# Nystrom attention and gated MLP on one core: identity products placed in other PSUM tiles, and four weight tiles of the second pair decoded elsewhere in ScalarE's order

## The chip, the cores and the metric

One core of a Trainium2 chip runs the whole program. The metric is the device time of one execution in microseconds; lower is better. The kernel before takes 792.78 us, the median of three runs (792.62 to 793.05).

## What is computed

Eight batches of eight heads, 576 tokens and 64 channels go through Nystrom attention with 32 landmarks, and the result, 4608 rows of 512, through a gated MLP of width 1536:

```python
q_lm, k_lm = means of q and k over 18 neighbouring tokens
A, Bm, C = softmax(q k_lm'), softmax(q_lm k_lm'), softmax(q_lm k')
Z = Bm' / (norm1(Bm) * norminf(Bm) + 1e-6)
for _ in range(6):
    Z = 2 * Z - Z @ Bm @ Z
x = A @ Z @ C @ v
xn = x / sqrt(mean(x * x) + 1e-6) * rms_g
out = (silu(xn @ w_gate) * (xn @ w_val)) @ w_out
```

## The kernel before

The program works batch by batch. For a batch the attention front makes the scores of the landmarks (`sC`, `sA`), exponentials (`E`, `tA`), the six Newton steps (`pn`, `PV`) and a small matrix `W`. The row norm needs the squares of `x` (`pO` on TensorE, `sq` on ScalarE), their sums (`pss`), which VectorE transposes (`sqT`), and a second small product (`pms`), from which a chain of VectorE operations (`ms`, `r`) makes the factor of each row. The scaled `AT` is split into a high and a low part, `an`.

The MLP does not multiply `x` by the gate and value weights directly. For each pair of 128-wide slices it first mixes the weights with the attention's matrix `WT` (`pM`, in `mix_weights`, L298), splits that into `Mhi` and `Mlo`, and then takes `an` times these: twelve products for each of four blocks of a pair, six into a gate bank `psg` and six into a value bank `psv`. ScalarE takes the SiLU of the gate bank (`s`, L533), VectorE multiplies by the value bank (L534). Three pairs make a half of the MLP, after which `outs` (L542) multiplies by `w_out` (`pso`).

Weights arrive as raw bytes and are decoded on the chip. `Weights.begin` (L177) puts two ScalarE operations on a tile (L195 and L197) and returns a function that puts the closing VectorE operation (L205). Four tiles make a pair of gate and value weights; the tiles of the first pair are `wgv0`, of the second `wgv1`, of the third `wgv2`. `opening` (L818) lays out batch 0 by hand: what is wrapped in `own` or `pin` keeps the order in which it is written, and the closing functions wait in the list `ends` until they are popped. `steady` (L966) then feeds the work of batch 1 into the first MLP chunk (`mlp`, L495), at block counts that `until` names, beside a stream of further weight tiles (`early.stream`). The order of instructions that nothing pins is set by the scheduler.

Products of the identity with itself have no use in the result; they keep TensorE at work. They go into free columns of a PSUM tile:

```python
        def idle(out, n):
            for _ in range(n):
                mm(out, ident, ident, start=True, stop=True)
```

There are three of them behind the sums of squares in `second` (L1154), in the last columns of the bank of `pss`, and six behind the mixing of the second pair in `mlp` (L512), in the last columns of the value bank `psv` of the block before.

Of the kernel before, what the change touches and what calls it, by code (L numbers as in the profile page):

```python
# [20 lines left out]
P = 128  # L21
# [39 lines left out]
def nystrom_moe_kernel(  # L61
# [53 lines left out]
    def mm(*args, **kw):  # L115
        tc.keep_in_program_order(nc.tensor.matmul(*args, **kw))  # L116
# [165 lines left out]
    def mixed_banks(wts, b, pair, banks=None):  # L282
        wgv = wts.get("gv", pair)
        pool, tag = banks or (pg, "pg")
        ps = [pool.tile([P, 4 * P], F32, name="pM", tag=tag) for g in range(G)]
        for h in range(4):
            for g in range(G):
                n = pos(g, h)
                mm(
                    ps[g][rows(n), :],  # L290
                    WT[half(h), b, 2 * g + h // 2, rows(n % 2)],
                    wgv[half(h), 2 * g + h // 2, :],
                    start=True,
                    stop=True,
                )
        return ps

    def mix_weights(wts, b, pair, late=False, own=free, banks=None):  # L298

        ps = mixed_banks(wts, b, pair, banks)  # L300
# [94 lines left out]
    hs, ends = [], []  # L395
# [99 lines left out]
    def mlp(wts, b, f0, an, store, part, following, after=2 * NF1):  # L495
# [4 lines left out]
        for n, pair in enumerate(pairs):  # L500
# [5 lines left out]
            for i in range(2):  # L506
                s = mp.tile([P, S], F32, name="s", tag="s", bufs=2)
                for e in range(2):
                    if very and i and e and n + 1 < NPAIR:
                        mix_weights(wts, b, pairs[n + 1])  # L510
                        if not n:
                            for _ in range(6):  # L512
                                mm(ps[:, 3 * P :], ident, ident, start=True, stop=True)
                        yield 1.1
# [63 lines left out]
    with tc.tile_pool(name="ap", bufs=1, side="right") as ap, tc.tile_pool(  # L578
# [158 lines left out]
        def expose(b, g, own=free):  # L737
            tA = state[b]["tA"][g]
            own(nc.scalar.activation(tA, tA, AF.Exp, scale=SC))
# [23 lines left out]
# [4 lines that stand above are left out]
# [51 lines left out]
        def opening():  # L818
# [53 lines left out]
            ends.append(early.begin(own))  # L872
# [4 lines left out]
            for _ in range(2):  # L877
                ends.pop(0)()
            next(parts)
            next(parts)  # L880
            for _ in range(2):
                ends.pop(0)()
            nxt.exps()
            next(parts)
            nxt.turned(es=(0,))
# [7 lines left out]
            nxt.turned(es=(1,))  # L893
# [72 lines left out]
        def steady(begun):  # L966
# [9 lines left out]
            expose(1, 0, pin)  # L976
            expose(1, 1, pin)
# [5 lines left out]
            yield 1.3, 0.0  # L983
            mix.add(early.stream(WAIT))
# [143 lines left out]
        def second(b, own=free):  # L1128
# [28 lines left out]
            if not b:  # L1157
                idle(room[:, 512 - P :], 3)
# [288 lines left out]
```

## Time and profile before

| | before |
|---|---|
| median of three runs | 792.78 us |
| profiled execution, time | 793.83 us |
| its span | 792.1 us |
| TensorE busy | 769.8 us (97%) |
| VectorE busy | 561.5 us (71%) |
| ScalarE busy | 418.2 us (53%) |
| mean granted TensorE clock | 0.991 |

The span goes from the first to the last instruction; 1.7 us of the profiled time lie around it. TensorE is busy for nearly all of the span, but not evenly: of the 40 slices of some 20 us on the page, the first three show 7, 7 and 6 tenths for it, every later one 9 and the last 8. A granted clock of 1.00 is 2.4 GHz and 0.50 is 1.2 GHz.

### The profile page before, as it was taken

Reading aid. Unit: us, or ns where it says so; the run is one execution under the profiler, and the core shown is the slowest. Engines: PE = TensorE matmul, PEld = TensorE weight load, DVE = VectorE, ACT = ScalarE, POOL = GpSimd, SP = SyncE. Lnnn points to the kernel's source line nnn. Section 1 sums busy time; section 2 is a strip of 40 time slices with the busy share of each in tenths; the row PEclk is TensorE's granted clock in tenths of the full one; section 3 lists DMA queues with packets and bytes.
Section 4 is the critical chain, followed back from the end, with each engine's and each line's share of the span. In section 5 each row is a group of like instructions: output and inputs, shape, how many; then the busy total and the mean of one; then the engine's idle time right before and its main releaser. Section 6 shows DMA issues by size and latency. Waiting matters only on the chain.

```text
span 792.1 us, 17966 instructions
## 1 busy us (share of the span) xinstructions
PE 769.8 (97%) x7042; PEld 619.4 (78%) x7042; DVE 561.5 (71%) x1325; ACT 418.2 (53%) x927; POOL 197.8 (25%) x211
## 2 busy tenths in 40 slices
PE   7769999999999999999999999999999999999998
PEld 5457768778778778678778879797979797979796
DVE  7696687957969758688577574767476757766672
ACT  4678365534545455464475785555355444535460
POOL 4524120110110200200200004353334424433430
PEclk9979999999999999999999999999999999999999
DMA  9966361541652541521556541334332424151412
GB/s 329 361 214 220 109 218 63 181 134 39 194 183 81 186 140 61 185 95 46 173 168 221 152 143 41 132 94 145 94 143 71 158 81 158 55 182 57 171 41 79
DMA packets 55204, 110.83 MB, mean 140 GB/s; under 512 B 5456, under 2 KB 29008, under 8 KB 55120
## 3 DMA queue, kind: packets, MB, share of 16 engines
q1 hardware_dynamic: 55120, 109.69, 41.1%
q8 instruction: 55, 0.90, 0.5%
q14 instruction: 29, 0.24, 0.1%
HBM read 73.69 MB, written 35.98 MB: 138 GB/s over the span
## 4 chain that ended last, share of the span: by engine, by line
PE 88%; ACT 4%; DMA 3%; DVE 3%; issue 1%; SPq 1%; POOL 1%; ACTq 0%; POOLq 0%
PE pso L116 38%; PE p L116 17%; PE psv L116 9%; PE psg L116 9%; PE pM L116 5%; PE pn L116 2%; PE sC L116 2%; PE pO L116 1%; DMA wrawg<-in_moe_w_gate_dram 1%; PE pCV L116 1%; DMA vt<-in_v_dram 1%; PE pss L116 1%; PE pW L116 1%; PE sE L129 1%; SPq L592 0%
## 5 line engine op out<-in xcount | busy, mean ns | idle before, releaser
L116 PE MATMUL pso<-wo,h 128*128 128x512 f32 x648 | 158.5, 396 | 0.0
L116 PEld LDWEIGHTS pso<-wo,h 128*128 128x128 f32 x648 | 118.6, 188 | 31.5 <-ACT E L685 4.2
L116 PE MATMUL pso<-lhio,h 128*128 128x512 f32 x432 | 139.3, 392 | 0.0
L116 PEld LDWEIGHTS pso<-lhio,h 128*128 128x128 f32 x432 | 81.1, 188 | 23.1 <-issue 5.9
L116 PE MATMUL p<-xb,Bwgv 128*128 128x288 f32 x560 | 90.8, 296 | 0.0
L116 PE MATMUL psg<-an,Mhi 128*128 128x288 f32 x384 | 85.8, 306 | 1.6 <-DVE Mlo L306 1.4
L116 PE MATMUL pso<-lloo,h 128*128 128x512 f32 x216 | 84.4, 391 | 0.0
L116 PE MATMUL psv<-an,Mhi 128*128 128x288 f32 x384 | 82.6, 299 | 0.0
L116 PEld LDWEIGHTS p<-xb,Bwgv 128*128 128x128 f32 x560 | 81.3, 188 | 1.1
L436 POOL TENSOR_TENSOR s<-s,vv 128x576 f32<-128x576 f32 x40 | 57.4, 1434 | 98.2 <-DVE vv L478 96.8
L116 PEld LDWEIGHTS psg<-an,Mhi 128*128 128x128 f32 x384 | 62.1, 190 | 12.9 <-DVE WT L1107 5.0
L116 PE MATMUL p<-xb,Bwo 128*128 128x288 f32 x392 | 70.1, 295 | 0.0
L116 PEld LDWEIGHTS psv<-an,Mhi 128*128 128x128 f32 x384 | 62.2, 189 | 1.8
L735 POOL TENSOR_TENSOR tA<-tA,mA 128x576 f32<-128x576 f32 x16 | 18.7, 1187 | 175.9 <-DVE mA L734 175.9
L1309 ACT COPY ob<-pso 128x512 f32<-128x512 f32 x36 | 21.1, 589 | 75.6 <-PE pso L116 50.7
L116 PEld LDWEIGHTS p<-xb,Bwo 128*128 128x128 f32 x392 | 58.9, 188 | 1.2
L533 ACT ACTIVATE s<-psg 128x288 f32<-128x288 f32 x96 | 39.4, 410 | 38.7 <-PE psg L116 38.5
L116 PE MATMUL psv<-an,Mlo 128*128 128x288 f32 x192 | 59.0, 307 | 0.0
L116 PE MATMUL psg<-an,Mlo 128*128 128x288 f32 x192 | 58.4, 304 | 0.0
L1371 DVE TENSOR_TENSOR obl<-obl,pso 128x512 f32<-128x512 f32 x36 | 24.7, 685 | 43.6 <-PE pso L116 42.9
L534 DVE TENSOR_TENSOR s<-s,psv 128x288 f32<-128x288 f32 x96 | 42.3, 446 | 16.7 <-PE psv L116 11.1
L538 ACT CAST h<-s 128x576 fp32r<-128x576 f32 x48 | 32.2, 670 | 27.5 <-DVE s L534 27.5
(206 smaller groups left out, 1488.6 us busy)
## 6 DMA issues: line engine op xcount, KB each, us to landing
xb<-ad SPq DMA_DIRECT2D x16, 1008.0 KB, 5.2
qk<-in_q_dram SPq DMA_DIRECT2D x16, 576.0 KB, 5.1
qk<-in_k_dram SPq DMA_DIRECT2D x16, 576.0 KB, 6.4
pd<-ob SPq DMA_DIRECT2D x36, 256.0 KB, 3.3
ad<-t SPq DMA_DIRECT2D x64, 144.0 KB, 1.8
obl<-pd SPq DMA_DIRECT2D x36, 256.0 KB, 2.7
out_dram<-obl SPq DMA_DIRECT2D x36, 256.0 KB, 2.0
vt<-in_v_dram SPq DMA_DIRECT2D x16, 512.0 KB, 5.6
```

The lines of the kernel that those rows point to most:

```text
L116: tc.keep_in_program_order(nc.tensor.matmul(*args, **kw))
L129: tc.keep_in_program_order(nc.tensor.transpose(*args))
L436: kept(eng.tensor_mul(ss[f][:, e], ss[f][:, e], vv[f][:, e]))
L533: silu["last"] = nc.scalar.activation(s[:, cols], banks[0], AF.Silu).ins
L534: nc.vector.tensor_mul(s[:, cols], s[:, cols], banks[1])
L538: nc.scalar.copy(h[:, 0, TAIL:], s)
L735: own(nc.gpsimd.tensor_sub(tA, tA, mA.unsqueeze(2).broadcast_to([P, NB, M])))
L1309: nc.scalar.copy(ob, ps)
L1371: kept(nc.vector.tensor_add(ob, ob, ps))
```

## The change

Identity products: the three behind the sums of squares go, the six in the value bank go, and eight new ones are put into the second bank of the mixing (`ps[1]`), ahead of the mixing of the second pair. The second pair's mixing is given priority in the scheduler. Of the second pair's four tiles, the first is decoded behind the exponentials of batch 1's first group instead of ahead of `W`, the second and third follow one place later each, and the fourth goes between the two exponentials `tA` of batch 1. Three closing operations of the first pair stand ahead of the two transposes of the sums, one behind them. The two transposes of batch 1's `sA` (`turned`) come together behind the first half's `an`. The stream of further weight tiles starts at block count 37 of the first chunk.

```diff
-    def mixed_banks(wts, b, pair, banks=None):
+    def mixed_banks(wts, b, pair, banks=None, fill=0):
         ps = [pool.tile([P, 4 * P], F32, name="pM", tag=tag) for g in range(G)]
+        for _ in range(fill):
+            mm(ps[1][:, :P], ident, ident, start=True, stop=True)
         for h in range(4):
...
-    def mix_weights(wts, b, pair, late=False, own=free, banks=None):
+    def mix_weights(wts, b, pair, late=False, own=free, banks=None, fill=0):
-        ps = mixed_banks(wts, b, pair, banks)
+        ps = mixed_banks(wts, b, pair, banks, fill)
...
                     if very and i and e and n + 1 < NPAIR:
-                        mix_weights(wts, b, pairs[n + 1])
-                        if not n:
-                            for _ in range(6):
-                                mm(ps[:, 3 * P :], ident, ident, start=True, stop=True)
+                        with nullcontext() if n else tc.high_priority():
+                            mix_weights(wts, b, pairs[n + 1], fill=0 if n else 8)
                         yield 1.1
...
             back(b, 1, own)
-            ends.append(early.begin(own))
             newton_weights(b, own)
             nxt.tops()
             parts = second(b, own)
             next(parts)
-            for _ in range(2):
+            for _ in range(3):
                 ends.pop(0)()
             next(parts)
             next(parts)
-            for _ in range(2):
-                ends.pop(0)()
             nxt.exps()
             next(parts)
-            nxt.turned(es=(0,))
+            ends.pop(0)()
             ends.append(early.begin(own))
             room = next(parts)
             low_parts = mix_weights(early, 0, 0, True, own, (pa, "pa"))
...
             next(parts)
-            nxt.turned(es=(1,))
+            nxt.turned()
             idle(room, 3)
...
             expose(1, 0, pin)
+            begun.insert(-1, early.begin(pin))
             expose(1, 1, pin)
...
             nxt.totals()
             yield 1.3, 0.0
+            yield from until(0, 37)
             mix.add(early.stream(WAIT))
...
-            if not b:
-                idle(room[:, 512 - P :], 3)
             yield 1.1, SQW
```

On ScalarE at the end of the opening, before (`wrawg2` is the first tile of the second pair, `wgv0` the first pair's weights):

```order
L197 ACTIVATE wgv0_462<-wrawg1_169 128x4x128
L195 ACTIVATE wrawv1_171<-wrawv1_171 128x512
L197 ACTIVATE wgv0_462<-wrawv1_171 128x4x128
L195 ACTIVATE wrawg2_176<-wrawg2_176 128x512
L197 ACTIVATE wgv1_584<-wrawg2_176 128x4x128
L1105 COPY W_592<-pW_587 128x128
```

and now:

```order
L197 ACTIVATE wgv0_462<-wrawg1_169 128x4x128
L195 ACTIVATE wrawv1_171<-wrawv1_171 128x512
L197 ACTIVATE wgv0_462<-wrawv1_171 128x4x128
L1104 COPY W_589<-pW_584 128x128
L1140 ACTIVATE sq_609<-pO_597 128x288
```

The tile `wrawg2` no longer stands ahead of the copy `W`, which the products `pO` read.

On VectorE at the sums of squares (`sqT` are the transposed sums, `ms` the start of the row factors, the four `wgv` rows the closing operations of the first pair), before:

```order
L205 SCALAR_TENSOR_TENSOR wgv_462<-wrawg_165,wgv_462 128x4x128
L205 SCALAR_TENSOR_TENSOR wgv_462<-wrawv_167,wgv_462 128x4x128
L1151 STREAM_TRANSPOSE sqT<-pss 128x288
L205 SCALAR_TENSOR_TENSOR wgv_462<-wrawg_169,wgv_462 128x4x128
L205 SCALAR_TENSOR_TENSOR wgv_462<-wrawv_171,wgv_462 128x4x128
L1151 STREAM_TRANSPOSE sqT<-pss 128x288
L717 STREAM_TRANSPOSE tA<-sA 128x288
L1164 TENSOR_SCALAR ms<-pms 128x18
```

and now:

```order
L205 SCALAR_TENSOR_TENSOR wgv_462<-wrawg_165,wgv_462 128x4x128
L205 SCALAR_TENSOR_TENSOR wgv_462<-wrawv_167,wgv_462 128x4x128
L205 SCALAR_TENSOR_TENSOR wgv_462<-wrawg_169,wgv_462 128x4x128
L1150 STREAM_TRANSPOSE sqT<-pss 128x288 x2
L205 SCALAR_TENSOR_TENSOR wgv_462<-wrawv_171,wgv_462 128x4x128
L1161 TENSOR_SCALAR ms<-pms 128x18
```

The two transposes of the sums follow each other, one closing operation stands behind them, and the transpose of `tA` is gone from here.

On ScalarE ahead of the first SiLU `s` (`tA` are batch 1's softmax terms, `wrawv3` the fourth tile of the second pair, `wrawg4` the first of the third), before:

```order
L195 ACTIVATE wrawv3_182<-wrawv3_182 128x512
L197 ACTIVATE wgv1_584<-wrawv3_182 128x4x128
L685 ACTIVATE E_781,ss_754<-sC_751,mx_753 128x288
L685 ACTIVATE E_781,ss_754<-sC_752,mx_753 128x288
L696 ACTIVATE eb_784,ss_754<-sC_752,mx_753 128x32
L739 ACTIVATE tA_659<-tA_659 128x576
L739 ACTIVATE tA_786<-tA_786 128x576
L979 ACT_TABLE_LOAD
L979 ACTIVATE tabled_794<-ones_80 128x1
L533 ACTIVATE s_734<-psg_735 128x288
L195 ACTIVATE wrawg4_422<-wrawg4_422 128x512
```

and now:

```order
L696 ACTIVATE eb_779,ss_749<-sC_747,mx_748 128x32
L739 ACTIVATE tA_699<-tA_699 128x576
L195 ACTIVATE wrawv3_182<-wrawv3_182 128x512
L197 ACTIVATE wgv1_653<-wrawv3_182 128x4x128
L739 ACTIVATE tA_781<-tA_781 128x576
L977 ACT_TABLE_LOAD
L977 ACTIVATE tabled_791<-ones_80 128x1
L533 ACTIVATE s_729<-psg_730 128x288
L533 ACTIVATE s_729<-psg_807 128x288
L533 ACTIVATE s_826<-psg_827 128x288
L195 ACTIVATE wrawg4_422<-wrawg4_422 128x512
L306 CAST Mhi_861<-pM_843 128x512
```

The fourth tile stands between the two exponentials of `tA`, no table load stands beside it, three SiLUs follow each other, and `Mhi` of the second pair comes behind one operation on a tile of the third pair.

## Rows read from the trace of the kernel before

**Rows 1.** Windows of the core by stretch (us, busy time and count of each engine, granted clock, DMA).

```profile
30.70:34.10 3.40, 3.40 (x32) 1.39 (x28) 2.05 (x4) 3.13 (x13) 2.54 (x4) 0.50 1.05 317
34.10:47.70 13.60, 11.91 (x116) 8.58 (x112) 12.13 (x36) 9.30 (x22) 1.90 (x2) 1.00 0.97 338
47.70:61.38 13.68, 7.13 (x41) 5.95 (x41) 11.01 (x32) 9.31 (x18) 3.75 (x4) 0.63 0.51 153
61.38:85.95 24.57, 23.23 (x339) 18.76 (x339) 19.31 (x41) 18.96 (x40) 10.83 (x14) 1.00 0.58 200
```

**Rows 2.** What TensorE waited for from 26 to 90 us (total, times, longest).

```profile
PE psv L116 <- DVE s L534: 3.9, 1, 3.9
...
PE pO L116 <- ACT W L1105: 2.2, 1, 2.2
...
PE psg L116 <- DVE Mlo L306: 0.6, 1, 0.6
```

**Rows 3.** Timeline of ScalarE, first stop (start, us, operation, idle before, releaser).

```profile
27.55 0.66 ACT L195 ACTIVATE wrawg<-wrawg 128x512 f32<-128x512 int8 x1 [3.08 <-DMA wrawg<-in_moe_w_gate_dram]
...
28.81 0.25 ACT L1105 COPY W<-pW 128x128 f32<-128x128 f32 x1
```

**Rows 4.** Timeline of TensorE from the first stop to pair 0, and batch 1's squares later.

```profile
29.11 3.34 PE L116 MATMUL pO<-AT,W 32*64 32x288 f32 x32 [2.23 <-ACT W L1105]
32.39 2.00 PE L116 MATMUL pss<-sq,ones 128*32 128x288 f32 x16
35.75 0.94 PE L116 MATMUL pss<-ident 128*128 128x128 f32 x6 [1.36 <-DVE sqT L1151]
36.52 0.29 PE L116 MATMUL pms<-sqT,sel 128*128 128x18 f32 x2
...
40.26 0.89 PE L116 MATMUL psg<-an,Mhi 128*128 128x288 f32 x2
...
89.22 1.18 PE L116 MATMUL pss<-sq,ones 128*32 128x288 f32 x16
```

**Rows 5.** Timeline of VectorE, same place.

```profile
34.05 0.65 DVE L205 SCALAR_TENSOR_TENSOR wgv<-wrawg,wgv 128x512 uint32<-128x512 uint32 x1
...
35.22 0.47 DVE L1151 STREAM_TRANSPOSE sqT<-pss 128x288 f32<-128x288 f32 x1
35.62 0.44 DVE L717 STREAM_TRANSPOSE tA<-sA 128x288 f32<-128x288 f32 x1
36.85 0.18 DVE L1164 TENSOR_SCALAR ms<-pms 128x18 f32<-128x18 f32 x1 [0.79 <-PE pms L116]
```

**Rows 6.** Timeline of TensorE around the second and third stop.

```profile
47.41 0.29 PE L116 MATMUL psv<-an,Mlo 128*128 128x288 f32 x1
50.39 1.51 PE L116 MATMUL pM<-wgv,WT 64*32 64x512 f32 x16 [2.69 <-DVE wgv L205]
55.77 2.93 PE L116 MATMUL psv<-ident 128*128 128x128 f32 x12 [3.86 <-DVE s L534]
58.35 0.83 PE L116 MATMUL psg<-an,Mhi 128*128 128x288 f32 x2
...
61.38 0.32 PE L116 MATMUL psg<-an,Mhi 128*128 128x288 f32 x1
...
71.26 1.09 PE L116 MATMUL pM<-wgv,WT 64*32 64x512 f32 x16
...
85.95 1.08 PE L116 MATMUL pso<-wo,h 128*128 128x512 f32 x4
```

**Rows 7.** Timeline of ScalarE ahead of the first SiLU.

```profile
48.53 0.68 ACT L739 ACTIVATE tA<-tA 128x576 f32<-128x576 f32 x1 [0.99 <-POOL tA L735]
49.22 1.28 ACT L979 ACT_TABLE_LOAD   x1
...
50.62 0.40 ACT L533 ACTIVATE s<-psg 128x288 f32<-128x288 f32 x1
```

**Rows 8.** DMA issues of the output weights (count, KB each, median us to landing).

```profile
wrawo<-in_moe_w_out_dram SPq DMA_DIRECT2D x12, 511.6 KB, 4.4
```

## Prediction

> **What bounds the kernel now.** I began with the page. Its slices show TensorE nearly always busy except in the first three, about the first 60 us, and the built program differs from the one before only in the first MLP chunk and ahead of it; from there on each engine has the same instructions in the same order. So whatever TensorE gains or loses until the products with `w_out` begin at 85.95 us [rows 6] is carried to the end, and I read that stretch alone. Four windows of it [rows 1] give a first answer: from 61.38 us TensorE is busy 23.23 of 24.57 us at a granted clock of 1.00 (2.4 GHz), but from 47.70 to 61.38 only 7.13 of 13.68 us at a mean of 0.63. The list of its waits and its timeline name three long ones [rows 2, 6]: 2.2 us for the copy `W`, 2.7 us for the closing decode of a weight tile, 3.9 us for a product of VectorE. The timelines of TensorE [rows 4, 6] place them: they end at 29.11, 50.39 and 55.77 us. The clock belongs to the same places: it is 0.50 (1.2 GHz) from 30.70 to 34.10, behind the first wait, and in part of 47.70 to 61.38, around the other two; between, with a wait of 1.36 us at 35.75, it stays at 1.00 [rows 1, 4].
>
> **The change, step by step.** All times are of the profiled execution, 793.83 us; the sum is made against it and then moved to the median, 792.78 us, which is 1.05 us lower.
>
> *The first tile of the second pair leaves the place ahead of `W`.* ScalarE stood until 27.55 us for that tile's DMA, then spent 1.26 us on it, and only then made `W` at 28.81 [rows 3]. TensorE had finished what `W` reads 2.23 us before `pO` starts at 29.11 [rows 4], that is at 26.88. Without the tile, `W` (0.25 us) ends at about 27.15 and `pO` starts at 27.2: **-1.9 us**. The tile now goes behind the exponentials, where it delays nothing that TensorE reads before the second pair.
>
> *Sums of squares.* Four things change between `pO` and `ms` at 36.85. The sums `pss` took 2.00 us at half clock; batch 1's take 1.18 [rows 4]. With the wait gone I expect the full clock: -0.8. Two closing decodes from 34.05 to 35.22 stood between the transposes [rows 5]: -1.2, of which 0.3 comes back because the second transpose then meets the end of the second half's sums. The three identity products from 35.75 to 36.52 [rows 4] go: -0.8. One decode of 0.65 returns ahead of `ms`, and 0.33 of it lies beside `pms`, from 36.52 to 36.85 [rows 4, 5]: +0.3. Together **-2.2 us**; pair 0's first product moves from 40.26 to about 36.2.
>
> *Both transposes of `sA` together.* The first, 0.44 us at 35.62, was hidden in the wait of 0.79 for `pms` [rows 5]. Now both stand between the halves of `an`, on the way to the second half: **+0.4 us**. TensorE ends the blocks ahead of the second pair at 44.0 where it was 47.70 [rows 6].
>
> *Mixing of the second pair.* Its wait of 2.69 us is for the fourth closing decode on VectorE, which moves with everything ahead of it. ScalarE's half of that tile takes 1.26 us in a gap of 0.99 [rows 3, 7], so ScalarE runs 0.3 late and VectorE, which still has three tiles to close, does not. The eight identity products take 8 x 0.26 = 2.1 us (three took 0.77 [rows 4]) and lie inside the wait: nothing; were the decode there at once, they would cost the 2.1. At full clock the mixing takes 1.09 instead of 1.51 [rows 6]: **-0.4 us**. It ends at 47.8 instead of 51.90.
>
> *Identity products out of the value bank.* From 51.90 to 61.38 TensorE waits 3.86 us, runs the six products for 2.58 (55.77 to 58.35) and then twelve real products in 3.03 at half clock [rows 6]. The wait is that for the bank which VectorE still reads [rows 2]; it goes, for the next products write other banks. At full clock the twelve take half, some 1.6. So 9.5 us become 1.6. What is late next: the first gate bank is free when the first SiLU has read it, which moves from 50.62 to about 47.2 [rows 7] and is early enough, and the second pair's first block needs `Mlo`, for which I put 0.7 us, the size of the one wait for `Mlo` in the list [rows 2]. Net **-7.2 us**: the second pair starts at 50.1 instead of 61.38.
>
> *What comes back.* While TensorE stood, ScalarE decoded three tiles of the third pair and VectorE closed three. That work now lies beside the second pair. From 47.70 to 85.95 VectorE has 11.01 + 19.31 = 30.3 us of work and ScalarE 28.3 [rows 1]. Moved 3.7 us forward at its start, VectorE alone lets the products with `w_out` begin no earlier than 44.0 + 30.3 = 74.3, so the whole gain there is at most 11.6. At the other end, three tiles of 1.26 us wholly on the path give back 3.8. In the stretch from 61.38 VectorE is 79% busy and TensorE idle for 1.3 us; with VectorE above 90% I take **+1.8 us** more. The SP queue's loads of these tiles each wait for a closing decode that frees the buffer and move with it. The later start of the weight stream only orders this work, and I cost it in this term.
>
> Sum: -1.9 - 2.2 + 0.4 - 0.4 - 7.2 + 1.8 = -9.5 us, so 784.3 for a profiled execution like the one shown and **783.3 us** for the median.
>
> *A decode between two exponentials.* The table load, 1.28 us [rows 7], comes behind both exponentials as before, and the built order has none beside the decode. If the decode's function needed a set of its own, two more loads, 2.6 us, would stand ahead of the first SiLU and the time would be 785.9 us; decodes alternate with exponentials in the built order before too with no load between, so I give this no chance. The Trainium skill, page "ScalarE: Activation LUTs", section "What ACT_TABLE_LOAD costs", gives 2.66 us in all, load and drain, for each switch to another set; an estimate from that page is 5.3 us for two and 788.6 us. The trace agrees with its 1.28 us for the load alone; no drain shows behind the one load that is there.
>
> **The rivals.**
>
> *The clock stays low at the second pair.* Half clock followed waits of 2.23 and 2.69 us, not one of 1.36 [rows 1, 4, 6]. After the change the longest gaps I expect are 1.3 at `pms` and 0.6 at the mixing, which speaks against it; for it speaks that without the three products two gaps follow each other closely at `pms`, and that behind six identity products the twelve of the second pair still took 3.03 us, in the stretch at a mean of 0.63. Price: 0.4 for the mixing and 1.5 for the twelve products: 792.78 - 7.6 = 785.2 us.
>
> *The decodes bind.* All 3.8 us of the three tiles come back instead of 1.8: 785.3 us. For it, VectorE's 30.3 us of work; against it, that TensorE reads the third pair some 10 us after the second.
>
> *The wait only changes its bank.* The new identity products write the bank in which batch 1's scores were; if it is still read until the decode is there, they run behind the wait and cost 2.1: 785.4 us. The last reader on ScalarE is done ahead of the first `tA`, before 48.53 less 3.7 [rows 7], so it is unlikely. It is also the case in which the change does not do what it says.
>
> *Slower: the output weights come one at a time.* The stream now starts later. If each `w_out` tile waited for the buffer of the one before, a tile would take 4.4 for its load [rows 8], 1.26 on ScalarE [rows 3] and 0.65 on VectorE [rows 5]: 6.3 us. Starting at about 50.1 + 3.8 + 4.4 = 58.3, the fifth is there at 89.8, while the products want it at about 76.4: 13.4 us of waiting against 9.5 gained, 796.7 us. From 5.5 us a tile (85.95 less 58.3, by five) this side wins. Against it: the raw ring has three buffers (`RAWS`), so two loads can be under way.
>
> **How the numbers follow.** A measurement of this kernel can tell about 0.2%, 1.6 us, from no change. Forecast 62%, clock 16%, binding decodes 11%, wrong bank 5%, slower 3%, and 3% that something I do not see eats the gain to within 1.6 us. The first four are faster by more than 1.6 us: 94%; same 3%, slower 3%. The range goes from the bound by VectorE, 792.78 - 11.6 = 781.2, to the clock's price and the full give-back together, 792.78 - 9.5 + 1.9 + 2.0 = 787.2.
>
> **What would show it.** `pO` starting near 27.2 with no wait for `W`; a granted clock of 1.00 from 30.7 us on; `pms` with no identity products ahead; the mixing of the second pair ending near 47.8 behind eight identity products; no wait of TensorE for VectorE's product behind it; the second pair's first block near 50 and the first `pso` near 76.5. I am wrong if TensorE still stands over 2 us ahead of the second pair, if the clock falls to 0.50 there, if waits for `Mlo`, `wgv` or `wo` of more than 4 us appear between 50 and 90 us, or if a difference arises behind the first chunk.

## The result and the profile after

The changed kernel takes 785.42 us, the median of four runs (785.27 to 786.52), beside 792.7 us for the kernel before in the same comparison: a ratio of 0.9911 with a 95% interval of 0.9894 to 0.9928, 7.3 us or 0.9% faster. The forecast was 783.3, so the sign, the place and most of the terms came out, and the time is 2.1 us above it. The profiled execution took 786.52 us, the longest of the four, with a span of 784.7.

The stretches of the profile after, by the same view as [rows 1] (columns: stretch, its length, busy time and count of TensorE, its weight loads, VectorE, ScalarE, GpSimd, granted clock, DMA share, GB/s):

```profile
27.45:48.72 21.27, 17.67 (x188) 11.67 (x187) 20.22 (x51) 17.07 (x44) 9.61 (x12) 1.00 1.01 351
48.72:60.55 11.83, 11.71 (x193) 9.78 (x187) 11.35 (x38) 9.82 (x22) 3.34 (x7) 1.00 0.51 177
60.55:63.39 2.84, 1.09 (x21) 0.18 (x17) 1.61 (x5) 1.39 (x3) 1.28 (x2) 1.00 1.04 349
63.39:77.36 13.97, 13.97 (x148) 11.95 (x149) 12.30 (x23) 12.00 (x23) 5.84 (x6) 0.88 0.61 174
```

The granted clock, 0.50 and 0.63 in two stretches of [rows 1], is 1.00 in the windows up to 63.39 us here. From 48.72 to 60.55 TensorE is busy 11.71 of 11.83 us and VectorE 11.35, 96%. Two things are new: 2.84 us ahead of 63.39 in which TensorE works for 1.09, and a clock of 0.88 behind it.

From the list of TensorE's waits from 26 to 90 us (total, times, longest), to be read against [rows 2]:

```profile
PE psg L116 <- DVE s L534: 1.7, 1, 1.7
...
PE psg L116 <- DVE tA L717: 0.5, 1, 0.5
```

Of the three long waits two are gone. The one for `W` fell from 2.23 to 0.35 us (the timeline below has it), the one of 3.86 ahead of the identity products in the value bank no longer exists, and that for the closing decode, 2.69 before, stands at 0.92 because the eight identity products now lie in it. In their place stands a wait of 1.75 us for a product `s`. It lies behind the third pair's mixing: the mixing of a pair stands ahead of the last of the four blocks of the pair before (`mlp`), so the twelve products behind it are still that pair's. In this sense the prediction and some expectations name a block "second pair" or "third pair" that is the last block of the pair before.

TensorE's timeline at the places of [rows 4] and [rows 6] (start, length, instruction, the idle time before it and what ended it):

```profile
27.85 2.82 PE L116 MATMUL pO<-AT,W 32*64 32x288 f32 x32 [0.35 <-ACT W L1104]
30.60 1.25 PE L116 MATMUL pss<-sq,ones 128*32 128x288 f32 x16
33.23 0.40 PE L116 MATMUL pms<-sqT,sel 128*128 128x18 f32 x2 [1.38 <-DVE sqT L1150]
...
44.83 1.95 PE L116 MATMUL pM<-ident 128*128 128x128 f32 x16
47.70 1.09 PE L116 MATMUL pM<-wgv,WT 64*32 64x512 f32 x16 [0.92 <-DVE wgv L205]
48.72 0.53 PE L116 MATMUL psg<-an,Mhi 128*128 128x288 f32 x2
...
50.42 0.30 PE L116 MATMUL psg<-an,Mhi 128*128 128x288 f32 x1
...
60.55 1.09 PE L116 MATMUL pM<-wgv,WT 64*32 64x512 f32 x16
63.39 0.68 PE L116 MATMUL psg<-an,Mhi 128*128 128x288 f32 x2 [1.75 <-DVE s L534]
...
77.36 1.09 PE L116 MATMUL pso<-wo,h 128*128 128x512 f32 x4
78.57 1.61 PE L116 MATMUL pO<-AT,W 32*64 32x288 f32 x16
...
81.79 1.57 PE L116 MATMUL pss<-sq,ones 128*32 128x288 f32 x16
```

Subtracting these starts from those of before gives how far ahead TensorE is: 1.26 us at `pO` (29.11 less 27.85), 3.29 at `pms`, 2.69 at the second pair's mixing, 9.63 at the product behind it (58.35 less 48.72) and 10.96 twelve products later (61.38 less 50.42). Then it shrinks: 10.71 at the third pair's mixing (71.26 less 60.55), 8.59 at the first `pso`, 7.43 at batch 1's sums (89.22 less 81.79). The spans differ by 7.4. So the change gained 11 us and gave 3.6 back between 50 and 82 us, 2.4 of it up to the first `pso` and 1.2 behind it. The opening of this execution was some 0.6 us late ahead of `pO` (29.11 less the wait of 2.23 is 26.88; 27.85 less 0.35 is 27.50), which hides that much of each lead.

ScalarE, at the places of [rows 3] and [rows 7]:

```profile
44.72 0.69 ACT L195 ACTIVATE wrawv<-wrawv 128x512 f32<-128x512 int8 x1
...
46.72 1.28 ACT L977 ACT_TABLE_LOAD   x1
...
49.54 1.09 ACT L306 CAST Mhi<-pM 128x512 fp32r<-128x512 f32 x2
```

The fourth tile's two operations begin at 44.72, right behind the first `tA`, the second `tA` follows at 46.03 and then the one table load: none stands beside the decode. `Mhi` of the second pair comes at 49.54, 0.8 us behind the mixing's end, early enough that TensorE never waits for it.

What ended the new wait, on VectorE first and on GpSimd behind it:

```profile
61.95 0.78 DVE L757 STREAM_TRANSPOSE AT<-tA 128x576 f32<-128x576 f32 x1 [1.23 <-POOL tA L752]
...
62.89 0.44 DVE L534 TENSOR_TENSOR s<-s,psv 128x288 f32<-128x288 f32 x1
```

```profile
58.06 1.16 POOL L752 TENSOR_TENSOR tA<-tA,rA 128x576 f32<-128x576 f32 x1 [1.91 <-DVE rA L751]
59.16 1.51 POOL L1067 COPY blocks<-Bs 32x64 f32<-32x64 f32 x4
60.76 1.16 POOL L752 TENSOR_TENSOR tA<-tA,rA 128x576 f32<-128x576 f32 x1
```

The product `s` at 62.89, which frees the bank for the block behind the third pair's mixing, stands behind the second transpose `AT`, for which VectorE stood 1.23 us because GpSimd did the four copies into `blocks` (59.16, 1.51 us) between its two products `tA` x `rA`. In the kernel before GpSimd did both products first, and VectorE stood idle beside them, for 2.82 us, because TensorE was only just behind its long stop:

```profile
58.17 2.27 POOL L752 TENSOR_TENSOR tA<-tA,rA 128x576 f32<-128x576 f32 x2 [2.67 <-DVE nsb L1044]
```

```profile
61.67 0.46 DVE L534 TENSOR_TENSOR s<-s,psv 128x288 f32<-128x288 f32 x1 [2.82 <-PE psv L116]
```

The second loss is on ScalarE:

```profile
76.26 0.68 ACT L195 ACTIVATE wrawo<-wrawo 128x512 f32<-128x512 int8 x1 [0.64 <-DMA wrawo<-in_moe_w_out_dram]
...
78.11 1.31 ACT L1140 ACTIVATE sq<-pO 128x288 f32<-128x288 f32 x4
```

Batch 1's squares `sq` start at 78.11, behind the decode of the sixth `w_out` tile, which itself stood 0.64 us for its load; TensorE's `pO` at 78.57 took 1.61 us where the kernel before took 0.74 (its second `pO`, at 86.96), and the sums 1.57 against 1.18 [rows 4].

### The profile page after: what moved, and what is told of

It is laid out like the page before. It is cut to its first block, busy times and chain, and to the rows that moved or that the text cites. A ratio compares the mean times of both kernels' runs of the same rounds, so it can differ in the third digit from the quotient of the medians.

```text
span 784.7 us, 17955 instructions
## 1 busy us (share of the span) xinstructions
PE 768.2 (98%) x7040; PEld 618.1 (79%) x7040; DVE 562.1 (72%) x1325; ACT 417.4 (53%) x927; POOL 197.9 (25%) x211
## 4 chain that ended last, share of the span: by engine, by line
PE 88%; DVE 4%; ACT 4%; DMA 2%; issue 1%; POOL 0%; SPq 0%; DVEq 0%; ACTq 0%
PE pso L116 38%; PE p L116 17%; PE psg L116 9%; PE psv L116 8%; PE pM L116 5%; PE pn L116 2%; PE sC L116 2%; PE pCV L116 2%; PE pO L116 1%; DMA qk<-in_k_dram 1%; PE pss L116 1%; PE pW L116 1%; PE sE L129 1%; DVE lmT L607 1%; DMA wrawo<-in_moe_w_out_dram 1%
```

## Experiments

Twelve experiments ran, each in four to twelve timed runs beside the kernel before, which had medians of 793.08 (experiments 1 to 4), 793.19 (5 to 8) and 793.17 us (9 to 12). Single executions of one kernel differ by 0.4 to 6 us, so times are compared by medians and steps by one profile each. Where an edit left the scheduler free, it changed the order of other engines too; this is said at the experiment.

**1. The first tile alone.** In the kernel before:

```diff
             back(b, 1, own)
-            ends.append(early.begin(own))
...
             nxt.turned(es=(0,))
-            ends.append(early.begin(own))
+            ends.extend(early.begin(own) for _ in range(2))
```

> The kernel before with one part of the change: the tile wrawg2 goes from ahead of W to behind batch 1's first exponentials, nothing else. My theory: the stop ahead of pO is that tile alone. pO starts about 1.8 us earlier against the end of its inputs (wait 0.4 instead of 2.2), the granted clock stays at 1.00 behind it, so the sums take 1.2 instead of 2.0, and the 2.6 us are kept to the end: about 790.1 us. Rival A, the later stops eat it: the second pair's decodes are bound by their loads and by ScalarE, so the waits of 2.7 and 3.9 us ahead of the second pair grow by what was gained: 792 to 793 us. Rival B, the clock does not depend on this stop: it falls at about 30 us all the same and only 1.8 us are gained: 790.9 us.

Measured: 791.29 us, ratio 0.9978 (0.9969 to 0.9987), 1.8 us faster than before. TensorE's timeline:

```profile
27.40 2.82 PE L116 MATMUL pO<-AT,W 32*64 32x288 f32 x32 [0.35 <-ACT W L1104]
30.15 1.25 PE L116 MATMUL pss<-sq,ones 128*32 128x288 f32 x16
33.57 0.94 PE L116 MATMUL pss<-ident 128*128 128x128 f32 x6 [2.16 <-DVE sqT L1150]
```

The wait for `W` is 0.35, and the sums take 1.25 us instead of 2.00, so the clock held. But the wait for `sqT` behind them grew from 1.36 [rows 4] to 2.16: the closing decodes on VectorE still stood between the two transposes. The lead of 2.24 us at the sums (32.39 less 30.15) is 2.18 at the identity products (35.75 less 33.57). The stop was that tile's, but the clock's 0.8 us is worth something only together with the new order on VectorE: the expected 790.1 was one term too low, rival A's 792 to 793 is out, and so is rival B, whose clock falls all the same.

**2 and 3. The six identity products taken out, and moved.** Both from the kernel before. Experiment 2 deletes them; experiment 3 puts eight into the mixing bank as the change does. ScalarE, VectorE and GpSimd have the same order in both. It is not that of the kernel before: with the six gone the scheduler also moved `ET`, tiles of the third pair and GpSimd's work behind the second pair's mixing. The edit of experiment 3:

```diff
-                        mix_weights(wts, b, pairs[n + 1])
-                        if not n:
-                            for _ in range(6):
-                                mm(ps[:, 3 * P :], ident, ident, start=True, stop=True)
+                        mix_weights(wts, b, pairs[n + 1], fill=0 if n else 8)
```

> The kernel before without the six identity products in the value bank, nothing put in their place. My theory: the stop of 3.86 us ahead of them and their own 2.6 us go, 6.4 us in all; the wait of 2.7 us for the decode stays idle, so the clock stays at 0.5 for the twelve products behind; some 3 to 4 us come back later, as in the changed kernel: 789 to 790 us. Rival A, the wait changes its bank: TensorE then waits for Mlo, or for the gate bank, for most of the 3.9 us, and about 792 us come out. Rival B, without give-back: 786.3 us.

> The kernel before with the six identity products replaced by eight in the second mixing bank ahead of the mixing, nothing else; against the run without the six, TensorE has eight identity products more in the idle time, and all other engines have the same order. My theory: they cost nothing, since the decode is waited for anyway, and keep the granted clock at 1.00 for the mixing and the twelve products, which gives 0.4 + 1.5 us: about 1.9 us faster than the run without the six, 787 to 788 us. Rival A, the clock has another cause, or the gain is given back at the next wait: the same as the run without the six within 0.4 us. Rival B, they run behind the decode: up to 2.1 us slower than that run.

Measured: 790.58 us without them (ratio 0.9972, 0.9963 to 0.9981), 789.85 with eight moved (0.9964, 0.9951 to 0.9978); I had expected 789 to 790 and 787 to 788. TensorE in experiment 2 (a run of 793.31, the longest of its twelve) and then in experiment 3 (789.12, the shortest of its seven):

```profile
50.46 1.80 PE L116 MATMUL pM<-wgv,WT 64*32 64x512 f32 x16 [2.70 <-DVE wgv L205]
```

```profile
49.50 1.09 PE L116 MATMUL pM<-wgv,WT 64*32 64x512 f32 x16 [0.92 <-DVE wgv L205]
...
54.18 0.40 PE L116 MATMUL psg<-an,Mhi 128*128 128x288 f32 x1 [1.79 <-ACT Mhi L306]
```

In experiment 2 the block behind the mixing starts at 52.19, 6.2 us earlier than before (58.35, [rows 6]); but the profiled execution has five waits of 0.4 to 1.3 us between 63 and 81 us, for products of VectorE and ScalarE, and the medians keep 2.5. In experiment 3 the mixing takes 1.09 us where it took 1.80 without the identity products, and then TensorE waits 1.79 us for `Mhi` (the rows name it), which on ScalarE stands behind decodes of the third pair's tiles, and later 1.76 and 1.22 us for products of VectorE. So what the clock gave is mostly a wait again: 0.7 us between the medians, with intervals that overlap, lies between the theory (1.9) and rival A (0.4). The stop at the value bank is worth 6 us at its place and only 2.5 to 3.2 at the end while the second pair's tiles are decoded where they were. Added to the 1.8 us of experiment 1 that is 5.0 of the 7.3; the rest comes with the other moves, which no run takes one by one.

**4. The six put back** into the changed kernel, behind the mixing, the eight kept.

```diff
                             mix_weights(wts, b, pairs[n + 1], fill=0 if n else 8)
+                        if not n:
+                            for _ in range(6):
+                                mm(ps[:, 3 * P :], ident, ident, start=True, stop=True)
```

> The changed kernel with the six identity products put back into the value bank behind the mixing (the eight ahead of it stay). In the changed kernel the mixing ends at 48.7 us and VectorE's last product that reads that bank ends at 50.7, so they would wait 2.0 us and run for 1.3 to 2.6 us. My theory: 3.3 to 4.6 us are lost at that place, but the later give-back of 3.9 us shrinks by about half, since VectorE and GpSimd get this time for batch 1: 786.5 to 788 us. Rival A, no give-back depends on it: 788.7 to 790 us. Rival B, the whole gain of that place goes (wait of 3.9 us, half clock): 793 us less the 4 us of the earlier steps, about 789 to 790 us, with a granted clock of 0.5 behind.

Measured: 790.1 us (787.59 to 793.74 in twelve runs), ratio 0.9968 (0.9952 to 0.9985): 4.7 us slower than the changed kernel. TensorE:

```profile
50.53 2.30 PE L116 MATMUL psv<-ident 128*128 128x128 f32 x12 [2.01 <-DVE s L537]
```

They wait 2.01 us and, with the products themselves, delay the next block by 4.0: it starts at 52.48, 5.05 us behind the mixing's start at 47.43, where the changed kernel needs 1.02 (48.72 less 47.70). I expected half of it to come back; none did by the medians, which are nearest to rival A (788.7 to 790). But the end does not price the six products alone. The scheduler also laid the later work of ScalarE, VectorE and GpSimd in another order; and the profile is that of the longest run, 793.74, with a further wait of 2.83 us for `Mlo` at 71.96 and a clock of 0.82 from 64 to 76 us, which take the whole lead: its first `pso` starts at 85.95 as before. The times follow the mean granted clock of each run: 787.59 and 787.87 at 1.000, 793.35 and 793.74 at 0.991. What makes the clock fall in some runs only stays open.

**5. The changed kernel again**, as a base for the rest.

> The changed kernel once more, beside its own variants. All theories: 785 to 786.5 us, the first product with w_out near 76.8 us (77.4 in the profile shown, in which the opening alone was 0.6 us late), one wait of TensorE of 1.0 to 1.8 us ahead of the third pair and batch 1's second pO stretched from 0.74 to 1.6 us.

Measured: 785.64 us (785.25 to 786.03), ratio 0.9907 (0.9893 to 0.9920). The wait of 1.75 us is there, at 63.08; the first `pso` starts at 76.19 and batch 1's sums at 80.12, so the lead falls from 9.76 to 9.10 between them (85.95 and 89.22 less these). The second `pO` took 1.29 us; I had expected 1.6.

**6. GpSimd's order.** In the changed kernel, batch 1's copies into `blocks` go behind both products `tA` x `rA`; in the built order VectorE's `Bs`, which they copy, comes two instructions later too, behind the second `rA`, and some work behind 64 us moves:

```diff
             inverse = next(start)
-            next(start, None)
...
             weigh(b, 1)
+            next(start, None)
```

> The changed kernel with one move on GpSimd: batch 1's copies into blocks go behind the second product tA x rA instead of between the two; TensorE's order is the same. My theory of the give-back: VectorE stood 1.23 us for the second tA with the product s of the gate bank queued behind it, and TensorE 1.75 us for that s, after which its clock fell for 3.3 us. With the move tA comes 1.5 us earlier, VectorE does not stand, TensorE's wait is 0.5 us or less and the clock stays at 1.00: 2 to 2.5 us earlier at the first product with w_out, of which up to 1.2 come back at batch 1's pO and sums, since ScalarE's squares stand behind decodes of w_out tiles: 783.2 to 784.5 us. Rival A, the decodes and loads of the third pair bind, as in the prediction's rival: no gain, 785.4 us. Rival B, blocks is needed soon after: slower by up to 1.5 us.

Measured: 785.11 us (784.84 to 785.29), ratio 0.9900 (0.9886 to 0.9913), 0.5 us below experiment 5 and above the 783.2 to 784.5 that I expected. TensorE, VectorE and GpSimd at the place:

```profile
60.90 0.53 PE L116 MATMUL pn<-PV 32*32 32x96 f32 x16 [1.22 <-DVE PV L1088]
...
62.85 0.53 PE L116 MATMUL psg<-an,Mhi 128*128 128x288 f32 x2 [0.40 <-DVE s L534]
```

```profile
57.93 1.07 DVE L1065 TENSOR_TENSOR Bs<-Bm,nden 128x64 f32<-128x64 f32 x1
58.92 1.66 DVE L205 SCALAR_TENSOR_TENSOR wgv<-wrawv,wgv 128x512 uint32<-128x512 uint32 x1
...
60.76 1.43 DVE L757 STREAM_TRANSPOSE AT<-tA 128x576 f32<-128x576 f32 x2
```

```profile
57.76 2.27 POOL L752 TENSOR_TENSOR tA<-tA,rA 128x576 f32<-128x576 f32 x2 [1.91 <-DVE rA L751]
```

VectorE no longer stands for the second `AT` (both follow at 60.76), but its product for `Bs` took 1.07 us instead of 0.17 in experiment 5, and the closing decode 1.66 instead of 1.21. Each ended as one of GpSimd's two products had ended: the one at 57.93 by 59.00, when GpSimd's first is over if each takes half of the 2.27, and the second at 60.58, 0.55 behind GpSimd's end at 60.03 (57.76 and 2.27). TensorE waits 1.22 us for a Newton step and 0.40 for `s` instead of 1.75 in one piece. The Trainium skill, page "SBUF — State Buffer", section "Who interferes with whom", says that a VectorE instruction with two inputs in SBUF and a GpSimd instruction that reads SBUF exclude each other, and that the later one stands for the whole of the earlier. By that rule `Bs` and the decode stand for the product of GpSimd that they meet, and the trace agrees in those two rows. The theory named the instruction that ended the wait, but not what the wait is made of: what VectorE gained (1.23 us) it lost beside GpSimd (0.90 and 0.45), and the block behind the mixing starts at 62.85 instead of 63.08. From 48.7 to 64 us VectorE is busy for 15.20 of 15.30 us here, 13.80 in experiment 5: with the order mended it has no time left. The first `pso`, at 75.38, is 0.81 us earlier than in experiment 5 (I had expected 2 to 2.5); then TensorE waits 0.80 us for the squares `sq` at 79.94, and 0.18 is left at the sums.

**7. Without the eight identity products** (`fill` is not passed; the other engines keep the order of the changed kernel).

> The changed kernel without its eight identity products; the order of all engines is otherwise the same. TensorE then stands 2.9 us ahead of the second pair's mixing. My theory: the clock falls there to 0.5, the mixing takes 1.5 instead of 1.1 and the second pair's twelve products 3.0 instead of 1.7, so 1.7 us are lost at that place; what TensorE loses there it gets back from the wait of 1.75 us ahead of the third pair, which is set by VectorE and GpSimd, so the time rises by 0 to 0.5 us: 785.4 to 786 us. Rival A, the loss is kept: 787.1 us. Rival B, the clock does not fall: 785.4 us with a granted clock of 1.00.

Measured: 787.37 us (786.6 to 787.93), ratio 0.9927 (0.9913 to 0.9941): 1.7 us slower than experiment 5. TensorE:

```profile
47.40 1.43 PE L116 MATMUL pM<-wgv,WT 64*32 64x512 f32 x16 [2.71 <-DVE wgv L205]
...
63.95 0.54 PE L116 MATMUL psg<-an,Mhi 128*128 128x288 f32 x2 [1.75 <-DVE s L534]
```

The wait ahead of the mixing is 2.71, the mixing takes 1.43, and the twelve products behind it run from 48.76 to 51.76, 3.0 us instead of 1.7. That is the price that I expected at the place, 1.6 us, but I thought that the later wait would absorb it. It did not: it is 1.75 us here too, and that block starts 0.87 us later than in experiment 5 (63.95 less 63.08), so half of the loss is left there. Behind it the clock is 0.86 from 64 to 76 us in this profile and 1.00 in that of experiment 5, which costs another 1.0 up to the first `pso` (14.13 us against 13.11) and which the changed kernel shows in some executions too. By the medians it is rival A, the loss kept; the profile shows half of it as a loss at the place. That the wait moves because batch 1's chain starts from TensorE's own products fits this, but no run shows it.

**8. The stream of tiles not held back** (the line with `until(0, 37)` deleted from the changed kernel).

> The changed kernel without the rule that holds the stream of further weight tiles back to block count 37. My theory: the third pair's tiles go among the first SiLUs again, Mhi of the second pair comes 1.5 to 2 us later, and TensorE waits for it ahead of the second pair's third block, as in the run with the eight moved products alone (1.79 us); since the w_out tiles come earlier too, the stretched pO of batch 1 (1.4 us) goes. Together within 0.8 us of the changed kernel: 784.8 to 786.2 us. Rival A, only the wait for Mhi: 787 to 787.5 us. Rival B, only the gain at pO: 784 us.

Measured: 785.95 us (785.38 to 787.63), ratio 0.9914 (0.9900 to 0.9928), the same as experiment 5 within the measurement. TensorE, in a profile of 787.63, the longest of its four runs:

```profile
54.73 0.65 PE L116 MATMUL pCV<-vt,ET 128*32 128x64 f32 x32 [2.07 <-ACT ET L791]
...
67.23 0.69 PE L116 MATMUL psv<-an,Mhi 128*128 128x288 f32 x2 [2.26 <-DVE s L534]
```

No wait for `Mhi`; instead 2.07 us for the copy `ET` and 2.26 for `s`, and batch 1's `pO` and sums no longer stretched. By the medians the amount was right (within 0.8 us); the place of the wait was not. An earlier stream moves TensorE's waits and gains nothing, so the later start is not the reason of the give-back.

**9. The three identity products behind the sums put back** into the changed kernel.

```diff
+            if not b:
+                idle(room[:, 512 - P :], 3)
             yield 1.1, SQW
```

> The changed kernel with the three identity products put back behind the sums of squares; all other orders stay. They write the bank that VectorE's transposes read, so they run behind the wait of 1.4 us, for 0.8 us. My theory: 0.6 to 0.8 us later at pms and from there to the end, since the run without the eight kept its whole loss: 786.2 to 786.5 us against 785.6. Rival A, VectorE's fourth closing decode ends 0.2 us behind pms anyway and hides part: within 0.3 us of the changed kernel. Rival B, without them the clock falls behind that wait (0.84 in the mean of 33 to 44 us in the second run of the changed kernel, 1.00 in the first), with them it does not: within 0.3 us, and a granted clock of 1.00 in every profile.

Measured: 786.57 us (785.23 to 787.05 in four runs), ratio 0.9917 (0.9902 to 0.9932). TensorE:

```profile
31.03 1.26 PE L116 MATMUL pss<-sq,ones 128*32 128x288 f32 x16
33.67 0.94 PE L116 MATMUL pss<-ident 128*128 128x128 f32 x6 [1.38 <-DVE sqT L1150]
34.44 0.29 PE L116 MATMUL pms<-sqT,sel 128*128 128x18 f32 x2
```

From the sums' start to `pms` it is 3.41 us (34.44 less 31.03) against 2.63 in the changed kernel (33.23 less 30.60): 0.78, the length of the three. The medians are 0.9 apart in the same direction (I expected 0.6 to 0.8), with intervals that overlap.

**10 to 12. What else is late.** Experiment 10 decodes the sixth `w_out` tile behind batch 1's squares; 11 adds the move of experiment 6; 12 also starts batch 1's Newton steps at block count 84 instead of 76. All from the changed kernel.

```diff
-            mix.add(early.stream(WAIT))
+            mix.add(early.stream(WAIT, 9))
...
-                    own(nc.scalar.activation(sq[:, n], po[n], AF.Square))
+                    made = own(nc.scalar.activation(sq[:, n], po[n], AF.Square))
+                if (b, e) == (1, 1):
+                    early.after = made.ins
```

> The changed kernel with the sixth w_out tile of batch 0 decoded behind batch 1's squares on ScalarE instead of ahead of them; TensorE's order is the same. My theory of the last part of the give-back: in the changed kernel the squares wait for that tile, and its load, by 1 to 2 us, so that batch 1's pO and sums stretch from 0.74 to 1.3 and from 1.18 to 1.57 and come 0.7 to 1.5 us late. With the move the sums start about 3.0 us behind the first product with w_out, as in the kernel before (3.3), instead of 3.9: 784.6 to 785 us. Rival A, the products with that tile now wait for it: 785.6 us or more. Rival B, something later binds: 785.6 us with the sums earlier all the same.

> Both moves in the changed kernel: batch 1's copies into blocks behind its second tA x rA, and the sixth w_out tile behind batch 1's squares. Alone the first gave 0.5 us (785.1), the 0.8 us that it was ahead at the first product with w_out being lost at the squares. My theory: with the squares free it keeps these: 784.0 to 784.5 us. Rival A, the products with the sixth tile wait: 785 us. Rival B, the step pn of batch 1, for which TensorE waited 1.2 us in the run with the first move alone, binds: 784.8 to 785.1 us.

> Both moves, and batch 1's six Newton steps start at block count 84 instead of 76, so that the second step, which waited 1.2 us for VectorE ahead of the third pair's mixing, comes behind that mixing. My theory: VectorE, busy for 97% of 48.7 to 60 us, is the bound there, so the wait turns into one of 0.8 to 1 us for the third pair's Mlo or s, and 0.2 to 0.7 us are gained against the run with both moves: 783.4 to 784.2 us. Rival, TensorE's order was the bound: 1.2 us gained, 783 us. Other rival: batch 1's end comes late and its sums wait: 785 us.

Measured: 784.91 us (784.8 to 785.26; ratio 0.9899, 0.9885 to 0.9914), 784.87 (784.08 to 785.59; 0.9895, 0.9878 to 0.9911) and 784.69 (783.37 to 785.97; 0.9896, 0.9881 to 0.9911). In experiment 10, TensorE:

```profile
76.50 1.08 PE L116 MATMUL pso<-wo,h 128*128 128x512 f32 x4
77.51 0.74 PE L116 MATMUL pO<-AT,W 32*64 32x288 f32 x16
...
79.76 1.18 PE L116 MATMUL pss<-sq,ones 128*32 128x288 f32 x16
```

The second `pO` and the sums are back at 0.74 and 1.18 us, the tile is decoded behind the squares at 79.59, and the lead no longer falls between the first `pso` and the sums: 9.45 (85.95 less 76.50) and 9.46 (89.22 less 79.76), where experiment 5 lost 0.66 and, at `pms` behind the sums, 1.0. Of this the medians keep 0.7, the time that I expected (784.6 to 785). The theory holds for this part, and with it the kernel is by the medians better than both that are compared here. Adding the other moves did not show in the medians: I had expected 784.0 to 784.5 of experiment 11, and it came out in the range of its rival B, the wait for the Newton step; of experiment 12 I had expected 783.4 to 784.2. From `pO` to batch 1's `pms`, a distance inside one profile, it is 56.01 us in experiment 5, 55.83 in 6, 54.94 in 10, 55.12 in 11 and 54.63 in 12. In experiment 12:

```profile
60.40 1.09 PE L116 MATMUL pM<-wgv,WT 64*32 64x512 f32 x16 [1.24 <-DVE wgv L205]
62.35 0.54 PE L116 MATMUL psg<-an,Mhi 128*128 128x288 f32 x2 [0.86 <-DVE s L534]
```

the wait of 1.22 us for the Newton step turned into one of 1.24 for the closing decode `wgv` of the third pair and 0.86 for `s`. VectorE is busy for 15.17 of 15.30 us from 48.7 to 64 us there. That speaks for VectorE, its standing beside GpSimd included, as the bound of that stretch, though the profiles of one execution each can't exclude more.

## Why the prediction was right, and where it was off

*The first tile.* Forecast -1.9; the wait fell by 1.88. Right, and experiment 1 shows it alone.

*Sums of squares.* Forecast -2.2, counted from `pO` to `ms`; that is 7.74 us before (36.85 less 29.11) and 5.83 after (33.68 less 27.85), -1.91. I had not seen what the third closing decode meets in its new place ahead of the transposes: GpSimd's `half` ran until 31.87 us (30.11 and 1.76), and the decode took 1.80 us, to 32.42, where one alone takes 0.65 [rows 5]. The sums had ended at 31.85 and the transposes began at 32.34, so some 0.5 us of TensorE's wait of 1.38 ahead of `pms` are this decode's.

```profile
30.62 1.80 DVE L205 SCALAR_TENSOR_TENSOR wgv<-wrawg,wgv 128x512 uint32<-128x512 uint32 x1
```

The three identity products were forecast at 0.8 and are 0.78 in experiment 9. What I costed as separate, the clock's 0.8, comes only with the closing decodes moved (experiment 1).

*Both transposes together.* Forecast +0.4; the list of waits after has 0.5 for `tA`, at 43.18, ahead of pair 0's third block, and the lead falls by 0.36 there (from 43.91 less 40.85 to 45.88 less 43.18). The size was right; the place is one block behind the one that I named.

*The mixing.* Forecast 1.09 us instead of 1.51 and eight identity products of 2.1 us inside the wait: 1.09, and 1.95 us with 0.92 of wait left. Right; experiment 7 prices them at 1.6 us at the place and 1.7 by the medians, against the 1.9 of the clock rival.

*The value bank.* Forecast that 9.5 us become 2.3, of which 0.7 for `Mlo`; they became 1.70 (48.72 to 50.42), since that wait did not come. A gain of 7.8 instead of 7.2. Experiment 4 shows the reverse at 4.0 us at the place, experiment 2 that the removal alone keeps 2.5.

*What comes back.* This is the term that was mis-sized: +1.8 in the forecast, 3.6 us in the profile of the result and 2.6 in that of experiment 5 (a lead of 11.22 at 50.16 us, a difference of the spans of 8.6). Up to the first `pso`, the stretch that I read, it was 2.4 and 1.5: the 1.8 was near, although I had taken it from VectorE's share (above 90%, measured 96%) without working it out. It is in the main the wait of 1.75 us for `s`. The row ahead of it is an order, a transpose that waits for GpSimd, but experiment 6 took that order away and 1.62 us of waits (1.22 and 0.40) came in its place, with VectorE busy all the time: VectorE's work, and what it stands for GpSimd, is the better account, which stays argued, as no run made either less. In the result's profile the clock fell behind that wait, worth 0.9 us more (below). What failed is the premise that a lead at the first `pso` is carried to the end: of 8.59 us there 7.4 were left, of 9.76 in experiment 5 8.6. These 1.2 us lie behind it, where I had put nothing; the squares behind the sixth `w_out` tile are 0.7 to 1.0 of them, which experiment 10 shows. My sentence that ScalarE's and VectorE's three tiles return beside the second pair was not tested by itself; experiment 8 shows that moving the stream earlier gains nothing.

*The rivals.* The low clock at the second pair did not come (1.00 from 48.72 to 63.39), and experiment 7 shows what it would have cost at the place. The sign that I gave, a clock of 1.00 from 30.7 us on, did not hold: it was 0.88 behind 63.39 in the result and 0.84 from 33 to 44 us in experiment 5. The rival of the binding decodes gave 785.3, the time that was measured. The squares' share does hang on a decode, of a `w_out` tile and not of the third pair's three; whether those three have a share in the wait of 1.75 us no run separates (in experiment 12 the closing decode of one is what TensorE waits for, 1.24 us). So the match of the number is not a proof, and the rival is not ruled out. The wait did not change its bank: the new identity products start at 44.83, right behind the last product of pair 0's third block, and wait for nothing. Output weights one at a time: ScalarE stands for such a load 0.90 us at the first tile (60.61) and 0.64 at the sixth, far from the rival's price of 13.4. No further table load came: the rows at 44.72 to 46.72 show one load of 1.28 us, as before. So the price of a switch by the Trainium skill, page "ScalarE: Activation LUTs", section "What ACT_TABLE_LOAD costs", had no second switch to act on. At the one that is there the next operation starts at 48.01, 0.01 us behind the load: no drain shows.

The forecast's shift from the profiled execution to the median (1.05 us lower) also mattered. Against the 784.3 us forecast for a profiled execution, the two profiles of the changed kernel are 786.52 and 785.25, of which the first lay 1.1 above the median of its runs, the second 0.4 below. The median of before rose to 793.1 in the later comparisons. So one profile and four runs leave the distance of 2.1 us uncertain by about 1 us.

## What to carry to other kernels

Identity products that keep TensorE at work belong in a bank whose last reader is done: in the right place eight of them were worth 1.6 us, in a bank that VectorE still read six cost 4.0, both at the place. When a stop of several us goes from the front of a chunk, look at what the other engines did beside it: here GpSimd's products and VectorE's waiting for them lay inside TensorE's stop and came out of it. An instruction that stands ahead of one that TensorE needs is the first thing to move, but it pays only if its engine has time left (experiments 6 and 10: 0.2 us and 1.1 us inside the profile). A later wait need not absorb an earlier loss whole: ask whether its cause starts from the engine that was delayed. And a lead is to be followed to the end of the program, not to the place where the order of instructions is the same again.

## What the runs showed of the hardware

The clock is not decided by the length of a wait alone. The changed kernel, in two executions with the same order and the same waits (1.38 and 1.39 us ahead of `pms`, 1.75 behind the third pair's mixing), had the low clock at different places; these are the two windows 33 to 44 and 64 to 76 us, of the profile of the result and then of experiment 5 (columns as above):

```profile
33.00:44.00 11.00, 9.86 (x100) 7.19 (x101) 10.33 (x32) 7.77 (x18) 2.92 (x5) 1.00 1.06 368
64.00:76.00 12.00, 12.00 (x139) 10.17 (x137) 11.02 (x22) 10.39 (x21) 5.84 (x6) 0.87 0.59 166
```

```profile
33.00:44.00 11.00, 10.46 (x102) 8.44 (x103) 10.33 (x32) 7.75 (x20) 2.74 (x5) 0.84 1.06 365
64.00:76.00 12.00, 11.69 (x143) 9.79 (x142) 11.21 (x21) 11.35 (x23) 5.78 (x6) 1.00 0.60 181
```

Here 1.00 and 0.87, there 0.84 and 1.00; a mean between the two levels, 1.00 and 0.50, is a window that was in part at the low one. In the ten profiles of the changed kernel and its variants, the wait ahead of `pms` or of its identity products is 1.37 to 1.39 us, and the first window has 1.00 in five and 0.84 in five (experiments 4, 5, 7, 11 and 12). Of the five profiles with the wait of 1.75 us, the second window is 0.86 or 0.87 in three (the result, experiments 7 and 9) and 1.00 in two (5 and 10). In the first window a fall costs nothing, as the wait for the closing decode behind it takes it up (the mixing starts at 47.70 and 47.42). In the second it goes on to the end: from the product behind the wait of 1.75 to the first `pso` it is 13.97 us in the profile of the result and 13.11 in experiment 5.

VectorE's closing decodes lengthen beside GpSimd. In the profiles of before, of the changed kernel and of experiments 5, 6, 7 and 12, between 26 and 84 us, every closing decode that took 0.85 us or more (up to 1.81, where one alone takes 0.65 to 0.7) had begun beside an operation of GpSimd on two tiles, and ended 0.54 to 0.56 us behind that operation.

The opening varies too. In the ten profiles of the changed kernel and of its variants, all alike up to `pO`, `pO` started between 27.10 us (experiment 12, a time of 783.37) and 28.53 (experiment 11, 785.59), with the same wait of 0.35 to 0.36 us ahead of it. This spread, 1.4 us, is as large as most of the effects studied here; a step is therefore better read as a distance inside one profile than as a difference of two times.
